# Moving the carry, one W product and the last sums of the early tiles from VectorE to GpSimd in an FFT plus state-space kernel

## The chip, the cores and the metric

The kernel runs on one core of a Trainium2 chip. The metric is the device time of one execution in microseconds (us). A core has TensorE (PE in the profile; PEld is its weight load), VectorE (DVE), ScalarE (ACT) and GpSimd (POOL), which run side by side and wait for each other on semaphores. SyncE (SP) issues most DMA transfers. All runs told here were of state fast unless the text says otherwise.

## The reference, cut to what matters

```python
# x: (1, 2048, 1024) bf16
X = rfft2(x);  a = irfft2(X * (w_r + 1j * w_i))      # branch A: a spectral filter with weights W
# branch B: a diagonal state-space model, h complex
h_t = Lam_bar * h_{t-1} + B_bar x_t                  # 2048 steps
b = 2 * Re(C h) + x * Dskip
out = g * a + (1 - g) * b                            # g = sigmoid(sum(x * gate_w))
```

## The kernel before

Both branches are matmuls on TensorE with VectorE work between them. The recurrence is cut in 8 chunks of 256 steps and two halves of the state, which makes 16 units. VectorE handles each unit in seven pieces: turn back, join, two scans, carry, turn, join on. The pieces lie in a list, and the program hands them out between other work by estimated cost (`owed`).

```python
def carry_on():                    # hands the last state of a chunk to the next chunk: 16 elements a partition
    if c + 1 < NCH:
        gl = u[:, :, :, TC - 1]
        nc.vector.tensor_mul(out=ck[:, 0, :, js], in0=gl, in1=cTC[:, js]...)
        nc.vector.tensor_mul(out=ck[:, 1, :, js], in0=gl[:, ::-1], in1=sTC2[:, :, js])
        nc.vector.tensor_add(out=carry[:, :, js], in0=ck[:, 0, :, js], in1=ck[:, 1, :, js])

def turn():                        # overwrites u, which carry_on reads
    nc.vector.tensor_mul(out=sg, in0=u[:, ::-1], in1=bc(3))
    nc.vector.tensor_mul(out=u, in0=u, in1=bc(2))
...
work.extend([(2.4, turn_back), (1.5, join), (2.3, lambda: scan(0)), (2.3, lambda: scan(1)),
             (0.5, carry_on), (2.4, turn), (1.4, join_on)])
```

The filter is applied in 16 groups. This stage, from the first inverse matmul (line L449) to the last, is called the W stage below. ScalarE casts X2 out of PSUM, VectorE makes two products, and TensorE multiplies both:

```python
def times_w(g, X2):
    V2 = gt.tile([P, 2, K], BF16, name="V2", tag="gv2", bufs=2)
    nc.vector.tensor_mul(out=V2, in0=X2, in1=Wb[g % 3][:, 1])     # L433
    nc.vector.tensor_mul(out=X2, in0=X2, in1=Wb[g % 3][:, 0])     # L434, in place
    return X2, V2
...
for g in range(16):
    X2s.append(s2(g + 2))
    # 4 matmuls on UV[0] (L449) and UV[1] (L450), then ScalarE casts to C1, which goes to DRAM
    yield "is1"
    UV = times_w(g + 1, X2s.pop(0))
```

Seven early tiles have their branch B in DRAM already. Near the end, each has it added:

```python
def late_tile(tb):
    ga, _ = spectral(tb, gB)
    for hf in range(2):
        nc.sync.dma_start(out=ye, in_=y_dram[tb, hf])
        nc.vector.tensor_add(out=ga[:, hf], in0=ye, in1=ga[:, hf])        # L581
    nc.sync.dma_start(out=out2[P * tb:P * (tb + 1), :], in_=...)          # L582
```

Of the kernel before, what the change touches and what calls it, by code (L numbers as in the profile page):

```python
# [23 lines left out]
P = 128  # L24
# [81 lines left out]
def kernel(  # L106
# [17 lines left out]
    nc = tc.nc  # L124
# [39 lines left out]
    ident = cpool.tile([P, P], BF16, name="ident")  # L164
# [47 lines left out]
    carry = cpool.tile([P, 2, 8], FP32, name="carry")  # L212
    ck = cpool.tile([P, 2, 2, 8], FP32, name="ck")
# [4 lines left out]
    def halloc(shape, dtype):  # L218
        pool = hpool[hcount[0] % (NHA + NHB) >= NHA]
        hcount[0] += 1  # L220
        return pool.tile(shape, dtype, name="h")
# [3 lines left out]
    def unit(c, q):  # L225
        sh = [P, 2, 4, TC]
        u = halloc(sh, BF16)
        js = slice(4 * q, 4 * q + 4)
        bc = lambda i: tab[:, i:i + 1, js, :].to_broadcast(sh)
        tmps = {}  # L230

        def turn_back():
            su = up.tile(sh, BF16, name="su")
            nc.vector.tensor_mul(out=su, in0=u[:, ::-1], in1=bc(1))  # L234
            nc.vector.tensor_mul(out=u, in0=u, in1=bc(0))  # L235
            tmps["su"] = su

        def join():
            su = tmps["su"]
            nc.vector.tensor_add(out=u[:, 0], in0=u[:, 0], in1=su[:, 0])  # L240
            nc.vector.tensor_sub(out=u[:, 1], in0=su[:, 1], in1=u[:, 1])
            if c:
                nc.vector.tensor_add(out=u[:, :, :, 0], in0=u[:, :, :, 0], in1=carry[:, :, js])

        def scan(ri):
            seg = u[:, ri].rearrange("p j t -> p (j t)")
            nc.vector.tensor_tensor_scan(out=seg, data0=rz[:, js].rearrange("p j t -> p (j t)"), data1=seg,  # L247
                                         initial=0.0, op0=ALU.mult, op1=ALU.add)

        def carry_on():  # L250
            if c + 1 < NCH:
                gl = u[:, :, :, TC - 1]
                nc.vector.tensor_mul(out=ck[:, 0, :, js], in0=gl, in1=cTC[:, js].unsqueeze(1).to_broadcast([P, 2, 4]))
                nc.vector.tensor_mul(out=ck[:, 1, :, js], in0=gl[:, ::-1], in1=sTC2[:, :, js])
                nc.vector.tensor_add(out=carry[:, :, js], in0=ck[:, 0, :, js], in1=ck[:, 1, :, js])

        def turn():
            sg = up.tile(sh, BF16, name="sg", tag="su")
            nc.vector.tensor_mul(out=sg, in0=u[:, ::-1], in1=bc(3))  # L259
            nc.vector.tensor_mul(out=u, in0=u, in1=bc(2))  # L260
            tmps["sg"] = sg

        def join_on():
            sg = tmps["sg"]
            nc.vector.tensor_add(out=u[:, 0], in0=u[:, 0], in1=sg[:, 0])
            nc.vector.tensor_sub(out=u[:, 1], in0=u[:, 1], in1=sg[:, 1])
            hs[c, q] = u

        for ri in range(2):
            psu = psU.tile([P, 4, TC], FP32, name="psu", tag="psu")  # L270
            for j in range(4):
                for d8 in range(8):
                    nc.tensor.matmul(psu[:, j, :], lhsT=BT[4 * q + j][:, ri, d8, :],  # L273
                                     rhs=xT[:, d8, TC * c:TC * (c + 1)], start=(d8 == 0), stop=(d8 == 7))
            nc.scalar.copy(out=u[:, ri], in_=psu)  # L275
            if ri == 1:
                work.extend([(2.4, turn_back), (1.5, join), (2.3, lambda: scan(0)), (2.3, lambda: scan(1)),
                             (0.5, carry_on), (2.4, turn), (1.4, join_on)])
            yield 3.5

    owed = [0.0]
# [17 lines left out]
    fft = {}  # L299

    def gfnet():
# [44 lines left out]
        Wb = fft["Wb"]  # L346
# [83 lines left out]

        def times_w(g, X2):
            V2 = gt.tile([P, 2, K], BF16, name="V2", tag="gv2", bufs=2)
            nc.vector.tensor_mul(out=V2, in0=X2, in1=Wb[g % 3][:, 1])  # L433
            nc.vector.tensor_mul(out=X2, in0=X2, in1=Wb[g % 3][:, 0])  # L434
            return X2, V2

# [2 lines left out]
        yield "s2"  # L439
        X2s.append(s2(1))  # L440
        UV = times_w(0, X2s.pop(0))
        yield "uv"
        for g in range(16):
# [42 lines left out]
    def after_ia():  # L486
        ictx.close()
        hpool[1] = ctx.enter_context(tc.tile_pool(name="hpB", bufs=NHB, side="right", reuse_waits="tile"))
        lp = ctx.enter_context(tc.tile_pool(name="lp", bufs=1, side="right", reuse_waits="tile"))
        fft["lp"] = lp  # L490
        fft["dgD"] = lp.tile([P, 8, P], BF16, name="dgD")
        for d8 in range(8):
            nc.vector.tensor_scalar_mul(out=fft["dgD"][:, d8, :], in0=ident, scalar1=dskT[:, d8:d8 + 1])
        fft["gt"] = bctx.enter_context(tc.tile_pool(name="gt", bufs=3, side="right", reuse_waits="tile"))
        fft["wp"] = bctx.enter_context(tc.tile_pool(name="wp", bufs=1, side="right", reuse_waits="tile"))
        fft["Sel"] = fft["wp"].tile([P, 4, P], BF16, name="Sel_sb")
        nc.sync.dma_start(out=fft["Sel"], in_=cKRS.rearrange("p (i m) -> p i m", m=P)[:, 2:6])
        fft["Wb"] = [fft["wp"].tile([P, 2, 2, K], BF16, name=f"Wb{i}") for i in range(3)]
        for w in fft["Wb"]:
            nc.gpsimd.memset(w[:, 0, :, 0:1], 1.0)  # L500
            nc.gpsimd.memset(w[:, 1, :, 0:1], 0.0)
# [54 lines left out]
    def spectral(tb, scale):  # L556
        ZT_t = fft["ZT"]
        pse = psU.tile([P, 4, H], FP32, name="ps_id", tag="psu")
        for slot, (cls, ri) in enumerate(((0, 0), (1, 1), (0, 1), (1, 0))):
            for kb in range(2):  # L560
                i = 4 * cls + 2 * kb + ri
                nc.tensor.matmul(pse[:, slot, :], lhsT=ZT_t[:, i, tb, :], rhs=fft["Gi"][:, i, :],  # L562
                                 start=(kb == 0), stop=(kb == 1))
        place[0] = (place[0] + 1) % 3
        at = 2 * D * place[0]
        part = raw[:, at:at + D].rearrange("p (s c n) -> p s c n", s=2, c=2)
        nc.scalar.activation(out=part.rearrange("p s c n -> p (s c) n"), in_=pse, func=ACT.Copy, scale=scale[:, tb:tb + 1])
        eo = raw[:, at + D:at + 2 * D].rearrange("p (c k) -> p c k", c=2)
        nc.vector.tensor_add(out=eo[:, :, 0:H], in0=part[:, 0], in1=part[:, 1])  # L569
        nc.vector.tensor_sub(out=eo[:, :, K - 1:H - 1:-1], in0=part[:, 0], in1=part[:, 1])  # L570
        ga = part.rearrange("p s c n -> p s (c n)")
        nc.vector.tensor_add(out=ga[:, 0], in0=eo[:, 0], in1=eo[:, 1])
        nc.vector.tensor_sub(out=ga[:, 1], in0=eo[:, 0], in1=eo[:, 1])
        return ga, eo

    def late_tile(tb):
        ga, _ = spectral(tb, gB)
        for hf in range(2):
            ye = fft["lp"].tile([P, K], FP32, name="yl", tag="ye", bufs=2)
            nc.sync.dma_start(out=ye, in_=y_dram[tb, hf])  # L580
            nc.vector.tensor_add(out=ga[:, hf], in0=ye, in1=ga[:, hf])  # L581
        nc.sync.dma_start(out=out2[P * tb:P * (tb + 1), :], in_=ga.rearrange("p h n -> p (h n)"))  # L582

    def own_tile(tb, ga):
# [30 lines left out]
    lre, lim, dskT = vecF[:, 0], vecF[:, 1], vecF[:, 3]  # L615
# [30 lines left out]
    cTC = sp.tile([P, 8], FP32, name="cTC"); nc.vector.tensor_mul(out=cTC, in0=c2c[:, 1], in1=r_sb)  # L646
    sTC2 = sp.tile([P, 2, 8], FP32, name="sTC2")
# [82 lines left out]
    for j in range(5):  # L730
# [15 lines left out]
    nc.vector.tensor_mul(out=grat, in0=grat, in1=gB)  # L746

    ssm = chain(unit(0, 0), unit(0, 1), unit(1, 0), unit(1, 1),
                early(0), unit(2, 0), early(1), unit(2, 1), early(2), unit(3, 0), early(3), unit(3, 1),
                early(4), unit(4, 0), early(5), unit(4, 1),  # L750
                early(6), unit(5, 0))
    for j in range(5, 16):
# [33 lines left out]
    ga = spectral(todo[0], grat)  # L786
    for n, tb in enumerate(todo):
        if units:
            for _ in unit(*units.pop(0)):
                vector(3.5)  # L790
        if n >= 2:
            late_tile(late.pop(0))
        ga_next = spectral(tb + 1, grat) if tb + 1 < 16 else None
        for _ in own_tile(tb, ga):
            vector(4.0)
        ga = ga_next
# [31 lines left out]
```

## Time and profile before

| | before |
|---|---|
| time, median of 3 runs | 374.31 us (372.9 to 374.5) |
| span of the profiled run | 371.7 us |
| busy: PE, DVE, ACT, POOL | 345.2, 290.2, 180.4, 19.3 us |
| W stage (first L449 to last L449) | 138.3 to 211.2, 72.9 us |
| from the W stage's end to the end of the span | 160.5 us |

The page of the profile, part 1 (busy time of each engine) and part 4 (the chain of work that ended last):

```profile
PE 345.2 (93%) x2499; PEld 236.3 (64%) x2527; DVE 290.2 (78%) x441; ACT 180.4 (49%) x225; POOL 19.3 (5%) x58
...
PE 73%; ACT 9%; DMA 8%; DVE 7%; issue 2%; SPq 1%; ACTq 0%; DVEq 0%
```

TensorE leads. But a share of the whole span hides how the stages differ. This is the table of busy time in two stretches, the W stage and all after it. Its columns are the stretch, its length, then busy us and number of instructions of PE, PEld, DVE, ACT and POOL, the granted TensorE clock, the DMA share and GB/s:

```profile
138.30:211.20 72.90, 72.48 (x466) 44.87 (x473) 70.48 (x91) 41.70 (x59) 0.00 (x0) 1.00 0.79 217
211.20:371.70 160.50, 152.54 (x1082) 104.29 (x1091) 121.49 (x174) 58.07 (x58) 0.00 (x0) 1.00 0.28 84
```

In the W stage two engines are full: PE 72.5 and DVE 70.5 of 72.9 us. VectorE has 2.4 us to spare there, and 39 us after it.

The groups of VectorE instructions that the change moves (line, engine, operation, output <- inputs, shapes, count, busy us, mean ns, idle before):

```profile
L433 DVE TENSOR_TENSOR V<-X,Wb 128x1024 bf16<-128x1024 bf16 x16 | 10.9, 679 | 1.0 <-ACT X L428 0.9
L581 DVE TENSOR_TENSOR raw<-yl,raw 128x512 bf16<-128x512 f32 x14 | 9.0, 685 | 0.0
L255 DVE TENSOR_TENSOR carry<-ck 128x8 f32<-128x8 f32 x14 | 2.3, 166 | 0.4
L253 DVE TENSOR_TENSOR ck<-h,cTC 128x8 f32<-128x8 bf16 x14 | 2.3, 165 | 0.3
L254 DVE TENSOR_TENSOR ck<-h,sTC 128x8 f32<-128x8 bf16 x14 | 2.2, 159 | 0.0
```

One stretch of the timeline of GpSimd, early in the kernel (start us, duration us, engine, line, operation). The same copy takes 0.40 us, then 1.44, then 1.35, then 0.39:

```profile
14.46 0.40 POOL L206 COPY rz<-r_sb 128x256 f32<-128x256 f32 x1
...
14.84 1.44 POOL L206 COPY rz<-r_sb 128x256 f32<-128x256 f32 x1
...
16.26 1.35 POOL L206 COPY rz<-r_sb 128x256 f32<-128x256 f32 x1
...
17.59 0.39 POOL L206 COPY rz<-r_sb 128x256 f32<-128x256 f32 x1
```

The chain of work shows VectorE making two-input sums at 14.88 to 16.02 us and at 16.02 to 17.35 us, just where the copies are long.

### The profile page before, as it was taken

The page shows a single profiled execution, that of the slowest core. Times are in us where ns is not written, and L with a number is a line of the kernel's source. Part 1 is how long each engine was busy: PE and PEld are TensorE (multiplying, and loading weights), DVE is VectorE, ACT ScalarE, POOL GpSimd, SP SyncE. Part 2 cuts the span into 40 slices and gives each one's busy share as a digit, 9 for nine tenths or more (in the row PEclk, how much of TensorE's full clock was granted, in tenths as well). Part 3 has the DMA queues.
Part 4 walks back from the last instruction along what each step waited for, and adds up shares of the span by engine and source line. Part 5 has one row for each costly group of instructions (what it writes and reads, how often), then busy time and mean ns, then how long its engine had stood idle before and what let it go on. Part 6 is the DMA issues. An engine that isn't in the chain of part 4 may idle for free.

```text
span 371.7 us, 6369 instructions
## 1 busy us (share of the span) xinstructions
PE 345.2 (93%) x2499; PEld 236.3 (64%) x2527; DVE 290.2 (78%) x441; ACT 180.4 (49%) x225; POOL 19.3 (5%) x58
## 2 busy tenths in 40 slices
PE   4968999899997999999999999889999999999995
PEld 3855656466766574747475759777758576755552
DVE  2695569539697899999999986774988999997442
ACT  2659899675412164656565416863224241432321
POOL 7600000100100000000000000000000000000000
PEclk9999999999999999999999999999999999999999
DMA  7999951599468547898993376630000213032341
GB/s 206 323 187 268 178 171 56 148 228 206 127 214 161 152 130 184 262 255 258 236 274 103 114 208 200 162 85 0 30 0 30 74 41 114 2 113 71 116 154 59
DMA packets 67775, 54.82 MB, mean 147 GB/s; under 512 B 39456, under 2 KB 56352, under 8 KB 67360
## 3 DMA queue, kind: packets, MB, share of 16 engines
q1 hardware_dynamic: 67312, 54.38, 54.6%
q0 software_dynamic: 352, 0.02, 0.8%
q8 instruction: 20, 0.33, 0.3%
q14 instruction: 11, 0.09, 0.1%
q10 hardware_dynamic: 80, 0.01, 0.0%
HBM read 29.74 MB, written 16.26 MB: 124 GB/s over the span
## 4 chain that ended last, share of the span: by engine, by line
PE 73%; ACT 9%; DMA 8%; DVE 7%; issue 2%; SPq 1%; ACTq 0%; DVEq 0%
PE psu L273 26%; PE ps_y L533 26%; PE ps_fd L310 6%; PE ps_id L562 3%; DMA BT<-in_A_x_dram 3%; ACT X L313 3%; DMA turn_scratch<-A 2%; PE ps_is L449 2%; PE ps_is L474 2%; ACT h L275 2%; PE ps_is L450 2%; PE ps_y L537 2%; PE ps_s L425 2%; DMA raw<-turn_scratch 1%; PE ps_y L540 1%
## 5 line engine op out<-in xcount | busy, mean ns | idle before, releaser
L273 PE MATMUL psu<-xT,BT 128*128 128x256 bf16 x1024 | 118.8, 274 | 1.4 <-DMA BT<-in_B_B_re_dram 1.4
L533 PE MATMUL ps_y<-CT,h 128*128 128x512 bf16 x496 | 113.2, 379 | 0.8
L273 PEld LDWEIGHTS <-BT 128*128 128x128 bf16 x1024 | 100.2, 98 | 19.1 <-DMA BT<-in_B_B_re_dram 1.8
L533 PEld LDWEIGHTS <-h 128*128 128x128 bf16 x512 | 49.9, 98 | 56.1
L247 DVE TENSOR_TENSOR_SCAN h<-rz,h 128x1024 bf16<-128x1024 f32 x32 | 72.1, 2280 | 0.3
L275 ACT CAST h<-psu 128x1024 bf16<-128x1024 f32 x32 | 32.3, 1010 | 62.7 <-PE psu L273 62.7
L234 DVE TENSOR_TENSOR su<-h,tab 128x2048 bf16<-128x2048 bf16 x16 | 19.6, 1224 | 29.1 <-ACT h L275 28.6
L591 ACT ACTIVATE raw<-ps_y,omg 128x1024 bf16<-128x1024 f32 x9 | 10.0, 1113 | 53.3 <-PE ps_y L540 53.3
L310 PE MATMUL ps_fd<-G_sb,preT 128*128 128x512 bf16 x122 | 29.8, 381 | 4.8 <-ACT X L313 3.9
L310 PEld LDWEIGHTS <-preT 128*128 128x128 bf16 x128 | 18.4, 145 | 13.5 <-issue 6.1
L313 ACT CAST X<-ps_fd 128x1024 bf16<-128x1024 f32 x16 | 20.7, 1305 | 7.4 <-PE ps_fd L310 7.3
L550 ACT ACTIVATE ye<-ps_y,omg 128x512 f32<-128x512 f32 x14 | 8.9, 683 | 29.1 <-PE ps_y L537 15.9
L427 ACT CAST X<-ps_s 128x1024 bf16<-128x1024 f32 x16 | 16.2, 1015 | 9.4 <-PE ps_s L425 9.4
L235 DVE TENSOR_TENSOR h<-h,tab 128x2048 bf16<-128x2048 bf16 x16 | 19.6, 1224 | 0.8
L260 DVE TENSOR_TENSOR h<-h,tab 128x2048 bf16<-128x2048 bf16 x16 | 19.6, 1224 | 0.5
L259 DVE TENSOR_TENSOR sg<-h,tab 128x2048 bf16<-128x2048 bf16 x16 | 19.5, 1219 | 0.1
L599 PE MATMUL pt<-ident,BT 128*128 128x128 bf16 x128 | 14.0, 292 | 4.9 <-DMA BT<-in_A_x_dram 4.9
L569 DVE TENSOR_TENSOR raw<-raw 128x512 bf16<-128x512 bf16 x16 | 6.7, 422 | 15.0 <-DMA out_dram<-raw 12.7
L562 PE MATMUL ps_id<-Gi_sb,ZT 128*128 128x256 bf16 x128 | 16.3, 273 | 1.4 <-ACT ZT L476 0.8
L474 PE MATMUL ps_is<-KRS_sb,raw 128*128 128x128 bf16 x128 | 15.4, 311 | 1.6 <-DMA raw<-turn_scratch 1.2
L476 ACT CAST ZT<-ps_is 128x1024 bf16<-128x1024 f32 x16 | 15.4, 1018 | 1.6 <-PE ps_is L474 1.6
L452 ACT CAST C<-ps_is 128x1024 bf16<-128x1024 f32 x16 | 16.1, 1006 | 0.0
(174 smaller groups left out, 399.1 us busy)
## 6 DMA issues: line engine op xcount, KB each, us to landing
BT<-in_A_x_dram SPq DMA_DIRECT2D x8, 512.0 KB, 6.2
turn_scratch<-A SPq DMA_DIRECT2D x16, 256.0 KB, 2.6
Bb<-turn_scratch SPq DMA_DIRECT2D x16, 256.0 KB, 4.5
turn_scratch<-C SPq DMA_DIRECT2D x16, 256.0 KB, 3.7
raw<-turn_scratch SPq DMA_DIRECT2D x16, 256.0 KB, 4.3
out_dram<-raw SPq DMA_DIRECT2D x16, 256.0 KB, 2.8
Wb<-in_A_w_r_dram SPq DMA_DIRECT2D x32, 127.8 KB, 4.0
Wb<-in_A_w_i_dram SPq DMA_DIRECT2D x32, 127.8 KB, 4.1
```

The source lines that it names most:

```text
L234: nc.vector.tensor_mul(out=su, in0=u[:, ::-1], in1=bc(1))
L235: nc.vector.tensor_mul(out=u, in0=u, in1=bc(0))
L247: nc.vector.tensor_tensor_scan(out=seg, data0=rz[:, js].rearrange("p j t -> p (j t)"), data1=seg, initial=0.0, op0=ALU.mult, op1=ALU.add)
L259: nc.vector.tensor_mul(out=sg, in0=u[:, ::-1], in1=bc(3))
L260: nc.vector.tensor_mul(out=u, in0=u, in1=bc(2))
L273: nc.tensor.matmul(psu[:, j, :], lhsT=BT[4 * q + j][:, ri, d8, :], rhs=xT[:, d8, TC * c:TC * (c + 1)], start=(d8 == 0), stop=(d8 == 7))
L275: nc.scalar.copy(out=u[:, ri], in_=psu)
L310: nc.tensor.matmul(ps[:, cls, :], lhsT=preT_A[:, cls, d4, j, :], rhs=G_sb[:, cls, d4, :], start=(d4 == 0), stop=(d4 == 3))
L313: nc.scalar.copy(out=X1.rearrange("p r (i c) -> p c r i", c=2), in_=ps.rearrange("p c (r i) -> p c r i", r=2))
L474: nc.tensor.matmul(pv[:, :, g::4], lhsT=Cq[:, g, P * kc:P * (kc + 1)], rhs=KRS_sb[:, 1, :], start=True, stop=True)
L533: nc.tensor.matmul(psy[:, 512 * dh:512 * (dh + 1)], lhsT=hs[c, jb // 4][:, ri, jb % 4, P * tq:P * (tq + 1)], rhs=CT[ri][:, jb, 512 * dh:51 ...
L562: nc.tensor.matmul(pse[:, slot, :], lhsT=ZT_t[:, i, tb, :], rhs=fft["Gi"][:, i, :], start=(kb == 0), stop=(kb == 1))
```

## The change

The intent is to relieve VectorE, busy 78% of the span, by an engine that is busy 5%.

```diff
         def carry_on():
-                nc.vector.tensor_mul(out=ck[:, 0, :, js], ...)
-                nc.vector.tensor_mul(out=ck[:, 1, :, js], ...)
-                nc.vector.tensor_add(out=carry[:, :, js], ...)
+                nc.gpsimd.tensor_mul(out=ck[:, 0, :, js], ...)
+                nc.gpsimd.tensor_mul(out=ck[:, 1, :, js], ...)
+                nc.gpsimd.tensor_add(out=carry[:, :, js], ...)
...
-                             (0.5, carry_on), (2.4, turn), (1.4, join_on)])
+                             (0.0, carry_on), (2.4, turn), (1.4, join_on)])
...
-            nc.vector.tensor_mul(out=V2, in0=X2, in1=Wb[g % 3][:, 1])
+            nc.gpsimd.tensor_mul(out=V2, in0=X2, in1=Wb[g % 3][:, 1])
...
-            nc.vector.tensor_scalar_mul(out=fft["dgD"][:, d8, :], in0=ident, scalar1=dskT[:, d8:d8 + 1])
+            nc.gpsimd.tensor_scalar_mul(out=fft["dgD"][:, d8, :], in0=ident, scalar1=dskT[:, d8:d8 + 1])
...
-            nc.vector.tensor_add(out=ga[:, hf], in0=ye, in1=ga[:, hf])
+            nc.gpsimd.tensor_add(out=ga[:, hf], in0=ye, in1=ga[:, hf])
```

The eight small `dgD` products (a diagonal matrix for Dskip) move as well. No work is removed.

More of the change, by code (lines that the diff above doesn't have):

```diff
@@ L252, in carry_on @@
                 gl = u[:, :, :, TC - 1]
-                nc.vector.tensor_mul(out=ck[:, 0, :, js], in0=gl, in1=cTC[:, js].unsqueeze(1).to_broadcast([P, 2, 4]))
-                nc.vector.tensor_mul(out=ck[:, 1, :, js], in0=gl[:, ::-1], in1=sTC2[:, :, js])
-                nc.vector.tensor_add(out=carry[:, :, js], in0=ck[:, 0, :, js], in1=ck[:, 1, :, js])
+                nc.gpsimd.tensor_mul(out=ck[:, 0, :, js], in0=gl, in1=cTC[:, js].unsqueeze(1).to_broadcast([P, 2, 4]))
+                nc.gpsimd.tensor_mul(out=ck[:, 1, :, js], in0=gl[:, ::-1], in1=sTC2[:, :, js])
+                nc.gpsimd.tensor_add(out=carry[:, :, js], in0=ck[:, 0, :, js], in1=ck[:, 1, :, js])
         def turn():
```

## The prediction

> **What bounds the kernel now.** The page: PE 345.2 us of 371.7 (93%), DVE 290.2 (78%), POOL 19.3. The chain that ended last is 73% PE, 7% DVE; its DVE pieces lie before 30 us, near 43, and at 126 to 134 us. From 130 us on PE is busy 9.9 of 10 us (table by windows), except at 230 to 250 us, and no PE wait in the list of waits is for DVE there. Freeing VectorE buys at most 1 or 2 us.
>
> But VectorE has no room where the W products are: from 130 to 200 us it is busy 9.3 to 9.9 of 10 us. In the timeline DVE needs about 4.48 us per W group, PE about 4.8. Product 1 ends 2.2 us ahead of PE's use of it, product 15 6 us ahead. That is all the slack of the stage.
>
> **What moves** (groups by form): V2, 16 x 0.68 us; carry, 42 x 0.16; late sums, 14 x 0.69; dgD, 8 x 0.25. VectorE loses about 28 us.
>
> **What it costs.** No POOL op in the trace has two full inputs. The Trainium skill, GPSIMD Engine Reference, section Performance versus the Vector engine, gives 4497 ns for a two-input add of 2048 fp32 elements. Estimate from it: V2 (1024 elements) 2.3 us, a late sum (512) 1.2 us. A carry op 0.25 us (POOL copies of 2 elements take 0.18 us undisturbed).
>
> This does not run beside VectorE. The skill, SBUF — State Buffer, says of the shared port pair that a VectorE op with two SBUF inputs and a GpSimd op that reads SBUF exclude each other. The trace agrees: a POOL copy to rz takes 0.39 us alone, 1.44 and 1.35 us where DVE's preT sums (1.2 us) run; an Acol copy 0.18 us alone, 0.95 us beside two DVE joins. Every VectorE op of the W stage has two SBUF inputs. So I count POOL's time as VectorE's.
>
> V2 gives DVE 0.68 us back per group and takes 2.3: 4.48 + 1.65, or about 6.2 us per group with carry, against PE's 4.8. The first product is also written in place over V2's input, so VectorE must wait for POOL's read. Over 15 groups 15 x 1.4 = 21 us, less 2 us initial slack: +19. The turn after each scan overwrites what carry reads, so it waits for two POOL ops: +0.3 us each, a few in this stage: +2. Late sums: 14 x 0.5 to 0.8 = 7 to 11 us more DVE time in 255 to 350 us, where DVE has some 10 us idle, and later output transfers, on which ACT and DVE already wait 5.3 and 12.7 us: +2 to 4. dgD, and carry queued behind POOL work that waits on DMA near 111 us: 0 to +2.
>
> **Predicted: 399 us, 8 in 10 between 382 and 414. Faster by over 2%: 0.03; within 2%: 0.12; slower by over 2%: 0.85.**
>
> **What would show it.** V2 on POOL at 2 us or more. The W stage, 137 to 210 us, lengthens to about 93 us, PE's busy share falls to about 8 of 10, PE waits about 20 us for is1 operands (X or V). DVE waits for V2 or has longer ops than before (scan over 2.28 us, products over 0.69, 1.22). After the stage, nearly the same length.
>
> **What would make it wrong.** If the lock doesn't hold for whole instructions, V2 overlaps and the time stays at 372 to 375 us. If bf16 makes V2 1.5 us, about 382. If POOL is starved until VectorE stalls, or V2 takes over 3 us, 410 or more. A late stage without slack adds up to 8 us.

## The result and the profile after

The kernel after takes 392.7 us (median of 4 runs, 390.66 to 396.7; the slowest of them was slow, and the median of the three fast ones is 391.54), against 373.61 us before (4 runs). The ratio is 1.0495, 95% interval 1.0425 to 1.0565: slower.

The page of the kernel after, the same two lines:

```profile
PE 351.1 (90%) x2527; PEld 235.0 (60%) x2527; DVE 299.8 (77%) x361; ACT 181.0 (46%) x225; POOL 115.7 (30%) x138
...
PE 41%; DVE 25%; DMA 10%; POOL 8%; ACT 8%; issue 5%; SPq 1%; POOLq 0%; DVEq 0%; ACTq 0%
```

VectorE has 80 instructions fewer and yet is busy 9.6 us more. The W stage and what comes after it:

```profile
139.80:227.10 87.30, 78.43 (x472) 45.74 (x473) 78.43 (x60) 40.24 (x56) 40.30 (x25) 0.94 0.69 180
227.10:389.40 162.30, 153.10 (x1093) 104.33 (x1091) 121.93 (x145) 58.41 (x58) 32.08 (x31) 1.00 0.28 84
```

The span grew by 17.7 us: the W stage by 14.4 (72.9 to 87.3), the part after it by 1.8, the part before it by 1.5. In the fast profiled runs the W stage starts anywhere between 136.3 and 143.3 us. Two runs of one and the same kernel, carry alone, have 136.3 and 141.6 us, so I read nothing from 1.5 us there.

The groups by shape, now. V is on POOL, X is the product left on VectorE (0.69 us before). L260 is the turn that overwrites what carry reads:

```profile
L433 POOL TENSOR_TENSOR V<-X,Wb 128x1024 bf16<-128x1024 bf16 x16 | 39.3, 2467 | 23.8 <-ACT X L428 11.1 <-PE ps_is L450 6.5 <-DMA Wb<-in_A_w_i_dram 3.5
L581 POOL TENSOR_TENSOR raw<-yl,raw 128x512 bf16<-128x512 f32 x14 | 17.4, 1265 | 59.2 <-DVE raw L572 42.4 <-ACT raw L591 10.6 <-DVE raw L573 6.1
L434 DVE TENSOR_TENSOR X<-X,Wb 128x1024 bf16<-128x1024 bf16 x16 | 28.1, 1759 | 10.7 <-POOL V L433 10.7
L260 DVE TENSOR_TENSOR h<-h,tab 128x2048 bf16<-128x2048 bf16 x16 | 19.6, 1225 | 3.3 <-POOL ck L254 3.0
```

The X product went from 692 to 1759 ns although nothing about it changed, and VectorE waits another 10.7 us for V before it. One such place in the timeline of the kernel after, first GpSimd, then VectorE:

```profile
157.40 0.20 POOL L253 TENSOR_TENSOR ck<-h,cTC 128x8 f32<-128x8 bf16 x1 [7.05 <-DVE h L247]
157.56 0.21 POOL L254 TENSOR_TENSOR ck<-h,sTC 128x8 f32<-128x8 bf16 x1
157.85 0.20 POOL L255 TENSOR_TENSOR carry<-ck 128x8 f32<-128x8 f32 x1
158.01 4.20 POOL L433 TENSOR_TENSOR V<-X,Wb 128x1024 bf16<-128x1024 bf16 x2
```

```profile
152.86 4.47 DVE L247 TENSOR_TENSOR_SCAN h<-rz,h 128x1024 bf16<-128x1024 f32 x2
160.16 2.59 DVE L434 TENSOR_TENSOR X<-X,Wb 128x1024 bf16<-128x1024 bf16 x1 [2.84 <-POOL V L433]
```

In this timeline GpSimd takes its instructions in the order of the program. The next two V products stand behind carry in that order, and carry waits for both scans. The first V needs an X2 that ScalarE had finished at about 153.4 us, but it starts at 158.0. VectorE has nothing to do meanwhile and waits 2.84 us. When the first V (2.1 us, half of 4.20) is done, the X product starts beside the second V and lasts until 162.75 us, 0.54 us after that V ends at 162.21.

So two mechanisms are in sight: VectorE's ops grow long while GpSimd works, and VectorE waits for a V that stands in a queue. The experiments separate them.

### The profile page after: what moved, and what is told of

Same layout as the page of the kernel before. It is cut to its first block, busy times and chain, and to the rows that moved or that the text cites. A ratio compares the mean times of both kernels' runs of the same rounds, so it can differ in the third digit from the quotient of the medians.

```text
span 389.4 us, 6432 instructions
## 1 busy us (share of the span) xinstructions
PE 351.1 (90%) x2527; PEld 235.0 (60%) x2527; DVE 299.8 (77%) x361; ACT 181.0 (46%) x225; POOL 115.7 (30%) x138
## 4 chain that ended last, share of the span: by engine, by line
PE 41%; DVE 25%; DMA 10%; POOL 8%; ACT 8%; issue 5%; SPq 1%; POOLq 0%; DVEq 0%; ACTq 0%
PE psu L273 16%; PE ps_y L533 11%; DVE X L434 6%; PE ps_fd L310 5%; DVE h L247 5%; DMA out_dram<-raw 3%; POOL dgD L493 3%; ACT X L313 3%; POOL raw L581 2%; POOL V L433 2%; DMA BT<-in_A_x_dram 2%; PE ps_is L474 2%; DVE su L234 2%; ACT h L275 1%; PE ps_id L562 1%
## 5 line engine op out<-in xcount | busy, mean ns | idle before, releaser
L533 PE MATMUL ps_y<-CT,h 128*128 128x512 bf16 x512 | 119.0, 387 | 0.0
L247 DVE TENSOR_TENSOR_SCAN h<-rz,h 128x1024 bf16<-128x1024 f32 x32 | 73.8, 2341 | 0.2
L253 POOL TENSOR_TENSOR ck<-h,cTC 128x8 f32<-128x8 bf16 x14 | 11.7, 833 | 122.7 <-DVE h L247 122.7
L433 POOL TENSOR_TENSOR V<-X,Wb 128x1024 bf16<-128x1024 bf16 x16 | 39.3, 2467 | 23.8 <-ACT X L428 11.1
L434 DVE TENSOR_TENSOR X<-X,Wb 128x1024 bf16<-128x1024 bf16 x16 | 28.1, 1759 | 10.7 <-POOL V L433 10.7
L581 POOL TENSOR_TENSOR raw<-yl,raw 128x512 bf16<-128x512 f32 x14 | 17.4, 1265 | 59.2 <-DVE raw L572 42.4
L310 PE MATMUL ps_fd<-G_sb,preT 128*128 128x512 bf16 x128 | 31.0, 387 | 4.3 <-ACT X L313 3.9
L449 PE MATMUL ps_is<-X,raw 128*128 128x512 bf16 x32 | 13.1, 409 | 11.6 <-DVE X L434 9.8
L427 ACT CAST X<-ps_s 128x1024 bf16<-128x1024 f32 x16 | 16.2, 1014 | 15.6 <-PE ps_s L425 15.6
L569 DVE TENSOR_TENSOR raw<-raw 128x512 bf16<-128x512 bf16 x16 | 11.5, 721 | 13.8 <-DMA out_dram<-raw 11.4
L260 DVE TENSOR_TENSOR h<-h,tab 128x2048 bf16<-128x2048 bf16 x16 | 19.6, 1225 | 3.3 <-POOL ck L254 3.0
L235 DVE TENSOR_TENSOR h<-h,tab 128x2048 bf16<-128x2048 bf16 x16 | 21.4, 1341 | 0.8
```

The lines of the kernel that those rows point to most:

```text
L235: nc.vector.tensor_mul(out=u, in0=u, in1=bc(0))
L247: nc.vector.tensor_tensor_scan(out=seg, data0=rz[:, js].rearrange("p j t -> p (j t)"), data1=seg, initial=0.0, op0=ALU.mult, op1=ALU.add)
L310: nc.tensor.matmul(ps[:, cls, :], lhsT=preT_A[:, cls, d4, j, :], rhs=G_sb[:, cls, d4, :], start=(d4 == 0), stop=(d4 == 3))
L433: nc.gpsimd.tensor_mul(out=V2, in0=X2, in1=Wb[g % 3][:, 1])
L533: nc.tensor.matmul(psy[:, 512 * dh:512 * (dh + 1)], lhsT=hs[c, jb // 4][:, ri, jb % 4, P * tq:P * (tq + 1)], rhs=CT[ri][:, jb, 512 * dh:51 ...
L581: nc.gpsimd.tensor_add(out=ga[:, hf], in0=ye, in1=ga[:, hf])
```

## The experiments

The theory of the prediction, here the port theory: a GpSimd instruction that reads SBUF and a VectorE instruction with two SBUF inputs exclude each other for the length of an instruction, as the Trainium skill, SBUF — State Buffer, section Who interferes with whom, states. Rivals: VectorE loses time only because it waits on semaphores for GpSimd (X overwrites what V reads), or because V stands behind carry in GpSimd's queue. The W stage in the tables is read from the one profiled run of each; a matmul record is missing in some traces, and then the neighbouring L450 gives the end.

### Which part of the change costs the time

V2 alone: `times_w` as in the change, all else as before.

> The kernel before with V2 alone on GpSimd. Port theory (a GpSimd op with two inputs and a VectorE op with two inputs exclude each other for a whole instruction): the W stage pays 15 times about 1.3 us less 2 us of slack, so most of the loss is here: 385 to 391 us. Queue theory (V2 is late because it stands behind carry in GpSimd's queue): no carry is there, so at most 3 us over before, 374 to 377 us.

All but V2: carry, late sums and dgD on GpSimd, V2 back on VectorE.

> The kernel after with V2 back on VectorE, so carry, late sums and dgD on GpSimd. Port theory: 374 to 379 us (up to 5 us from waits of the turn for carry and from later output). If carry or the late sums were the loss: 385 us or more.

| kernel | median us | ratio to before, 95% | W stage us |
|---|---|---|---|
| after | 392.7 | 1.0495 (1.0425 to 1.0565) | 87.3 |
| V2 alone | 388.07 | 1.0358 (1.03 to 1.0416) | 83.0 |
| all but V2 | 376.1 | 1.0036 (0.9984 to 1.0088) | 72.9 |

V2 alone makes most of the loss, and the rest alone costs nothing that the runs resolve. The two parts add up to 3.9%, the change costs 5.0%: about one more per cent seems to exist only together. By the three intervals that difference is uncertain by about one per cent itself, so it is taken up again below.

The timeline of V2 alone, VectorE and then GpSimd, shows what V does to its neighbour:

```profile
145.90 2.08 DVE L253 TENSOR_TENSOR ck<-h,cTC 128x8 f32<-128x8 bf16 x1
147.91 0.15 DVE L254 TENSOR_TENSOR ck<-h,sTC 128x8 f32<-128x8 bf16 x1
...
151.18 0.68 DVE L265 TENSOR_TENSOR h<-h,sg 128x1024 bf16<-128x1024 bf16 x1
151.78 2.60 DVE L266 TENSOR_TENSOR h<-h,sg 128x1024 bf16<-128x1024 bf16 x1
```

```profile
145.43 2.53 POOL L433 TENSOR_TENSOR V<-X,Wb 128x1024 bf16<-128x1024 bf16 x1 [2.79 <-PE ps_is L450]
151.49 2.35 POOL L433 TENSOR_TENSOR V<-X,Wb 128x1024 bf16<-128x1024 bf16 x1 [3.53 <-ACT X L428]
```

A carry product of 16 elements, which takes 0.16 us, lasts 2.08 us: it ends at 147.98 us, and V at 147.96. A join of 0.68 us that has nothing to do with W lasts 2.60 us. The profile lists no wait on a semaphore for these ops; they have begun and stand still. In this run it happened to X products, carry, joins, a turn back and a scan: to whatever op began while V ran.

How long VectorE stands still can be counted between two points with the same work between them: from the end of the first X product to the end of the last. These are the windows of before and of V2 alone, with the columns of the table above:

```profile
137.57:204.73 67.16, 66.79 (x424) 40.76 (x429) 64.88 (x83) 39.49 (x55) 0.00 (x0) 1.00 0.82 220
143.20:224.45 81.25, 73.20 (x450) 43.21 (x458) 80.46 (x68) 40.30 (x55) 36.13 (x14) 0.98 0.72 190
```

VectorE has 68 instructions in the second window and the same 68 and 15 V in the first. Those 15 V took 10.2 us (15 x 0.68), so the 68 went from about 54.7 to 80.5 us: 25.8 us of standing still beside the 14 V that GpSimd made in that time, 1.84 us a V.

### Is it a wait on a semaphore?

Swap: VectorE makes its product first, into the second buffer; GpSimd makes its own in place afterwards. VectorE then never waits for GpSimd in this stage.

```diff
-            nc.vector.tensor_mul(out=V2, in0=X2, in1=Wb[g % 3][:, 1])
-            nc.vector.tensor_mul(out=X2, in0=X2, in1=Wb[g % 3][:, 0])
-            return X2, V2
+            nc.vector.tensor_mul(out=V2, in0=X2, in1=Wb[g % 3][:, 0])
+            nc.gpsimd.tensor_mul(out=X2, in0=X2, in1=Wb[g % 3][:, 1])
+            return V2, X2
```

> V2 alone moves, but VectorE now makes its product first, into the second buffer, and GpSimd makes its own in place after it, so VectorE never waits on a semaphore of GpSimd in this stage. Port theory: within 3 us of V2 alone, 385 to 391 us, with VectorE's ops lengthened. Wait theory (the loss is VectorE waiting for GpSimd to read the tile it overwrites): 373 to 378 us.

Measured: 386.67 us, ratio 1.0293 (1.0246 to 1.034), and 83.2 us from the first to the last L450 (the later operand here). The loss stays with VectorE's wait gone. By itself this doesn't settle it, since TensorE now waits for GpSimd's later product (8.7 us in 5 waits). The next two runs are cleaner, because nobody waits for the added work.

Added reads and added writes: the kernel before keeps its VectorE work, and GpSimd is given idle work of about 2 us a group, once with two SBUF inputs and once with none.

```diff
+            DM = gt.tile([P, K], BF16, name="DM", tag="gdm", bufs=1)
+            # added reads:
+            for h in range(2):
+                nc.gpsimd.tensor_mul(out=DM, in0=C1[:, h], in1=MT_sb...[:, 0:K])
+            # added writes, the other kernel:
+            nc.gpsimd.tensor_copy(out=DM[:, 0:2], in_=C1[:, 0, 0:2])
+            for _ in range(4):
+                nc.gpsimd.memset(DM, 0.0)
```

> The kernel before with its VectorE work unchanged, and in each of the 16 groups two added GpSimd multiplies of 512 elements with two inputs from SBUF, into a tile nobody reads; they follow ScalarE's cast of C1, and VectorE waits for none of them. About 2.1 us of GpSimd a group. Port theory: VectorE needs 4.5 + 2.1 = 6.6 us a group against TensorE's 4.8, so 15 x 1.8 less 2 to 6 us of slack: 393 to 400 us, with VectorE's ops lengthened. Wait theory and queue theory: as before, 372 to 375 us.

> As the run with added multiplies, but GpSimd does a copy of 2 elements (to be paced by C1 in the same way) and four memsets of 512 elements, about 2 us a group, which read nothing from SBUF. Port theory on reads: 372 to 375 us. If any GpSimd work of that length hurts (instruction traffic, write port, power): 385 us or more.

| kernel | median us | ratio to before, 95% | W stage us |
|---|---|---|---|
| added reads | 393.91 | 1.0503 (1.043 to 1.0577) | 91.5 |
| added writes | 372.63 | 0.9978 (0.9902 to 1.0054) | 72.8 |

The two products of VectorE by shape, with added reads, and then with added writes together with GpSimd's memsets:

```profile
L434 DVE TENSOR_TENSOR X<-X,Wb 128x1024 bf16<-128x1024 bf16 x16 | 21.1, 1316 | 0.5
...
L433 DVE TENSOR_TENSOR V<-X,Wb 128x1024 bf16<-128x1024 bf16 x16 | 18.3, 1144 | 0.0
```

```profile
L457 POOL MEMSET DM<- 128x512 bf16 x64 | 33.6, 525 | 3.7
...
L434 DVE TENSOR_TENSOR X<-X,Wb 128x1024 bf16<-128x1024 bf16 x16 | 11.1, 692 | 0.6
L433 DVE TENSOR_TENSOR V<-X,Wb 128x1024 bf16<-128x1024 bf16 x16 | 10.9, 679 | 1.0 <-DMA Wb<-in_A_w_i_dram 0.4 <-ACT X L428 0.4
```

Useless reads by GpSimd, on which no VectorE instruction waits, cost as much as the whole change, and the products take 1.7 and 1.9 times as long. 33.6 us of memsets in the same places leave the products at 692 and 679 ns, exactly as before. So it is neither a wait nor GpSimd's activity as such; it is GpSimd reading SBUF beside VectorE. Every VectorE op of this stage has two SBUF inputs; that an op with one input would be spared was not tested here. The copy of two elements in the writing kernel reads too, but it is short (0.2 us undisturbed).

### Half a dose

The first half of V2 on VectorE, the other on GpSimd.

```diff
-            nc.vector.tensor_mul(out=V2, in0=X2, in1=Wb[g % 3][:, 1])
+            nc.vector.tensor_mul(out=V2[:, 0], in0=X2[:, 0], in1=Wb[g % 3][:, 1, 0])
+            nc.gpsimd.tensor_mul(out=V2[:, 1], in0=X2[:, 1], in1=Wb[g % 3][:, 1, 1])
```

> V2 halved: its first 512 elements on VectorE, the other 512 on GpSimd, all else as before. Whole V2 on GpSimd held VectorE about 1.9 us a group; half should hold it about 0.9 us and save it 0.34 us. Port theory: 4.48 + 0.6 = 5.1 us a group against TensorE's 4.8, less slack of 2 us: 0 to 4 us over before, 373 to 378 us. If the loss were a fixed cost for each GpSimd op of the stage: near V2 alone, 385 us or more.

Measured: 378.2 us, ratio 1.0117 (1.007 to 1.0165), W stage 77.0 us. The stage grows by 4.1 us for half and by 10.1 us for all. In the window between the X products (137.08 to 212.84 us) VectorE is busy 73.6 us against 64.88 before. About 4 us of V had left it (15 x 0.27: 0.68 for a whole V less 0.41 for a half), so it stood still for 12.8 us, 0.9 us for each of 14 halves against 1.84 for a whole V. The cost follows the length of GpSimd's work; that each op costs the same whatever its length is ruled out. Half still loses 1.2%: less than the 2% that counts as slower here, but its interval leaves out 1.

### The per cent that exists only together

All but carry: the kernel after with carry back on VectorE, cost 0.5 as before. Then the same with the cost entry left at 0.0, so that pieces are handed out by the entry of the kernel after.

> The kernel after with carry back on VectorE, its cost entry as before. Port theory: a few us below the kernel after, 386 to 391 us, since the turn no longer waits and V2 still takes the port. Queue theory (V2 behind carry is the main loss): near before, 374 to 378 us.

> The kernel after with the three carry ops back on VectorE, but with carry's cost kept at 0.0 in the work list, so the order of pieces is that of the kernel after (the earlier run without carry on GpSimd had 0.5). W stage of the kernel after 87.3 us, of that earlier run 83.1 us. If the difference is V2 standing behind carry in GpSimd's queue: stage 82 to 84 us, time 386 to 389 us. If it is the order of VectorE's pieces that the cost entry sets: stage about 87 us, time 391 to 394 us.

| kernel | median us | ratio to before, 95% | W stage us | VectorE's wait for V, us |
|---|---|---|---|---|
| after | 392.7 | 1.0495 (1.0425 to 1.0565) | 87.3 | 10.7 (4 waits) |
| carry on VectorE, 0.5 | 387.18 | 1.0333 (1.0277 to 1.0389) | 83.1 | 1.9 |
| carry on VectorE, 0.0 | 388.06 | 1.0384 (1.0332 to 1.0437) | 85.4, in a slow run | 2.6 (1 wait) |

(Two of these medians include a slow run; of the fast runs alone they are 391.54 for after and 387.62 for the last kernel.) Taking carry out of GpSimd's queue wins back 1.1 to 1.6 points, each uncertain by about 0.9, and the 10.7 us of waits for V fall to 2 or 3. That agrees with V standing behind carry. The order of VectorE's pieces may hold up to half a per cent of it: the two ratios without carry overlap, and the second kernel's profile fell into a slow run, so its 85.4 us decides nothing. One thing more is not separated: in the kernel after the granted clock was 0.94 in the W stage (1.00 before). This is the W stage with carry on VectorE and cost 0.5:

```profile
140.50:223.60 83.10, 73.60 (x465) 44.23 (x474) 82.24 (x71) 40.68 (x56) 34.82 (x14) 1.00 0.72 189
```

TensorE idles there for 9.5 us (83.10 - 73.60), no less than in the kernel after (8.9 us). What differs is its busy time, 73.60 against 78.43 us. In the kernel after some groups of matmuls come after a longer stop and are slow, as the first of this stage, which takes 0.59 us where the median of this line is 0.38:

```profile
139.80 0.59 PE L449 MATMUL ps_is<-X,raw 128*128 128x512 bf16 x1 [2.71 <-DVE X L434]
```

From 140 to 144 us the granted clock was 0.64. So that the queue costs about 4 us of the stage agrees with these runs, but whether it does so by VectorE's waits or by fewer, longer stops of TensorE with a lower clock after them stays open.

### Do the small parts win by themselves?

Carry alone on GpSimd with cost 0.0; late sums alone; then carry alone again with more rounds, and the cost entry alone with nothing moved.

> The kernel before with carry alone on GpSimd, with the change's cost of 0.0 in the work list. Both theories: within 2 us of before plus what the turn waits for it, 373 to 377 us.

> The kernel before with the late sums alone on GpSimd. My prediction: 2 to 4 us over before, 375 to 378 us. If the slack of the late stage holds them: 373 to 375 us.

> Carry alone on GpSimd, as in the earlier look (ratio 0.994, interval 0.989 to 0.9995), with more rounds: is it a version that beats before? If real: 0.991 to 0.997. If that was chance: interval around 1.000.

> The kernel before with carry's cost set to 0.0 in the work list and nothing moved. If a gain of carry alone comes from the order of pieces: the same ratio as carry alone. If from carry leaving VectorE: 1.000.

| kernel | rounds | median us | ratio to before, 95% |
|---|---|---|---|
| carry alone | 3 | 372.49 | 0.9944 (0.9893 to 0.9995) |
| carry alone, again | 5 | 374.0 | 1.0003 (0.9961 to 1.0045) |
| cost 0.0 alone | 5 | 374.13 | 1.0018 (0.9973 to 1.0062) |
| late sums alone | 3 | 374.0 | 0.9986 (0.9933 to 1.0038) |

The first run of carry alone looked like a small gain, with an interval that just left out 1. The second, with more rounds, does not repeat it: 1.0003. No kernel beats before.

The late sums do cost something that three rounds can't resolve. After TensorE's last matmul the span goes on for 4.4 us before (367.3 to 371.7) and for 4.4 us with carry alone. With late sums on GpSimd it is 6.6 us (late alone), 6.8 us (all but V2) and 6.1 us (after). These are the last instructions of the chain of work with late sums alone, and of before:

```profile
366.00 0.43 DVE raw L572
366.56 1.21 POOL raw L581
367.76 1.11 POOLq L823
```

```profile
367.11 0.23 PE ps_y L540
367.37 1.11 ACT raw L591
```

The chain used to end with TensorE and ScalarE; now it ends with a GpSimd sum. In the timeline of SyncE in the kernel after, the last late tile's output is issued at 385.53 us, and the last own tile's, which is behind it in the queue, only at 385.96. Elsewhere in the late stage VectorE pays for the same port (L569 and L570 rise from 422 and 418 ns to 781 and 776 ns with late sums alone, 11.5 us for 2 x 16 ops), but it had 39 us of idle time there, and the time of that kernel did not grow (0.9986).

## Why the prediction was right

The measured 392.7 us lies in the range of 382 to 414, and the direction and the cause were right. Point by point:

- **What bounds.** TensorE bounds, with VectorE just as full in the W stage: right. Freeing VectorE bought nothing measurable (carry alone 1.0003).
- **The port.** VectorE and GpSimd exclude each other: right, shown by added reads (1.0503) against added writes (0.9978).
- **V2's size.** This is the term that was mis-sized. The prediction had 2.3 us for V, all of it lost by VectorE: 1.65 us net a group, about 25 us in 15 groups, and +19 us for the stage after slack. Two V in a row took 4.20 us, so 2.10 each. And VectorE does not lose all of that: with V2 alone it stood still for 1.84 us a V, 25.8 us in all, while 10.2 us of V left it. That is 15.6 us net instead of 25. These 9 us are what the stage fell short by: it grew by 10.1 us instead of 19.
- **Carry.** +2 us was expected, from the turn waiting for two carry ops (listed at 3.0 us in the kernel after). That wait alone cost no time (carry alone 1.0003). What goes with about 4 us more in the W stage beside V2, and what the prediction missed, is the order of GpSimd's queue: carry waits for the scans and V waits behind carry. By which way it costs them is open, as said above. The prediction thought of carry behind other work, near 111 us, not of V behind carry.
- **Late sums.** +2 to 4 us was expected; about 2 us appear, at the very end of the span of the profiled runs; the times of late sums alone do not resolve them.
- **dgD and the start.** Not resolved in the time: the start of the W stage moves by more than this from run to run. But the timeline of the kernel after shows the queue that the prediction feared. The eight dgD products took 11.0 us on GpSimd, from 0.60 us each up to 2.59 where VectorE had a scan of 2.29 us under way: here GpSimd is the one that stood still. Carry stood behind them, and a turn waited 0.96 us for it at 107 us.
- **The signs named.** V at 2 us or more: yes, 2.10. The W stage at 93 us: 87.3. PE's waits of 20 us for operands: 11.6 us are listed (9.8 for X, 1.8 for X2). The stage's 14.4 us are 8.5 us more idle PE (72.90 - 72.48 = 0.4 before, 87.30 - 78.43 = 8.9 after) and 6.0 us more busy PE (72.48 to 78.43) at a granted clock of 0.94. So PE's share fell only to 9 of 10, because slower matmuls count as busy.

So the errors were on both sides and in part cancelled: V2 too dear by 9 us, carry beside V2 too cheap by about 2. That the second error took 2 us off the first was luck.

The Trainium skill pointed to the outcome. GPSIMD Engine Reference, section Engine selection, sends elementwise work to VectorE and calls GpSimd about 2 times slower for two inputs; here V went from 0.68 to 2.10 us, 3.1 times. Perfetto Trace Analysis, section Optimizing Scalar/DVE Operations, warns that since the two share an SBUF read port, moving work between them might not help; here it cost 3.6% for V2 alone.

## What to carry to other kernels

An engine that is idle is not free if it shares a port with the busy one: count the time of a two-input GpSimd op as time that VectorE loses from the two-input op beside it (1.84 of 2.10 us here), and move work only where it is short or where VectorE has slack. A moved instruction also joins another engine's queue: look at what stands in front of it there and what that waits for. And before a small gain is believed, run it again with more rounds.

## What the Trainium skill lacked or had wrong

- GPSIMD Engine Reference, section Performance versus the Vector engine: it has a measured figure for fp32 alone (2048 elements, 4497 ns). The runs show 2.10 us for a bf16 multiply of 1024 elements (two in 4.20 us): nearly the same time per element (2.05 against 2.20 ns), so bf16 brought GpSimd little, while VectorE takes 0.68 us for it. For a sum with one fp32 and one bf16 input of 512 elements it shows 1.2 us.
- SBUF — State Buffer, section Who interferes with whom: agrees. Two-input VectorE ops stand still beside GpSimd reads (0.68 becomes 2.60 us, 0.16 becomes 2.08 us), and writes alone do not matter (33.6 us of memsets, products unchanged at 692 and 679 ns). What it lacks is how much of the GpSimd time VectorE loses in a full schedule: 1.84 of 2.10 us a V here.
- That GpSimd's queue is in order the skill does state (PSUM — Partial Sum Buffer, section Engine vs sequencer instructions). No page has what this costs when work is moved there: V behind carry gave 10.7 us of VectorE waits in 4 places, against 1.9 us without carry in that queue.
